# Keeping converted first-layer weight parts in DRAM and reading them back for the second token batch

## The chip, the cores and the metric

One core of a Trainium2 chip runs the kernel. The metric is device time in microseconds for one execution. Three runs of the kernel before took 870.82, 871.75 and 873.16 us; the median is 871.75 us.

## What is computed

Attention with a bucket mask (a key counts only where its six sign bits equal those of the query) over 2 batches, 8 heads, 768 positions of 64 numbers, and then two MLPs in a row on the 1536 x 512 result. Weights come as float64.

```python
q_bits = (np.einsum('bhsd,dk->bhsk', q, proj) > 0)      # k_bits alike; a bucket is its 6 bits
scores = np.where(q_bucket == k_bucket, scale * q @ k.T, -1e9)
attn = softmax(scores);  x = (attn @ v)                  # 1536 tokens x 512
h = x @ w_in;   x = (h * sigmoid(1.702 * h)) @ w_out     # first MLP,  512 -> 2048 -> 512
h = x @ w_in2;  out = (h * sigmoid(h)) @ w_out2          # second MLP, 512 -> 2048 -> 512
```

## The kernel before, in words

**Numbers.** TensorE works on float32r, so every operand is split into a high and a low part, and each product is three matmuls. The weights need more: they are float64, 8 bytes each, read as pairs of 32-bit words. For a block of 128 hidden units, `Weights.step` makes from the `raw` words a float32 tile `f` and then the parts `hi` and `lo`. That takes one ScalarE instruction (line 152), four VectorE instructions (lines 153, 154, 155, 157), a ScalarE copy that makes `hi` (line 159) and a GpSimd subtraction that makes `lo` (line 160). A block has kind "i" (128 columns of `w_in`) or "o" (128 rows of `w_out`); the two kinds of one block of hidden units form a place in the stream. A raw block is 512 KB, each of its two parts 256 KB.

**The stream of weights.** `order` lists 45 places: the 16 of the first MLP for the first token batch, then 13 of the same 16 again for the second batch (12 down to 0; the last three are still in SBUF), then the 16 of the second MLP. So 13 places, 26 blocks, are fetched and converted twice. Parts live in rings: `wpool` has room for 3 places, and once attention's memory is free, a pool `w2` for 6 more. A place's tiles can be written when the place that held them before has been used. `fetch` issues the transfer of a raw block on SP's queue (line 127), some blocks ahead; there are 2 raw tiles, 4 once attention is done.

**The stages.** Attention works through the heads in 96 steps, 48 for each batch. A step is the scores on TensorE, their minimum on VectorE (line 407), the exponential on ScalarE (412), a split into float16 parts (423 or 421, and 427 on GpSimd), and for every two steps one transposing DMA on SP (433, `pt<-hl`) whose result TensorE multiplies by v (445 to 447). Beside the second batch's attention the first MLP runs on the first batch's tokens (token blocks 0 and 1 of 384): `gemm1` is line 593, the gate (lines 598 to 604) is made on ScalarE, VectorE and GpSimd, `gemm2` is line 627, and its results are added up in `part` (634, 636). When attention is over, the first MLP runs on blocks 2 and 3 in units of places: the three that are still there, then 4, 4, 4 and 1. Then the second MLP takes all four blocks through units of four places.

**What sets the order.** The program calls its tasks in one order, each with a head start in instructions (`SOONER`), and a scheduler then writes each engine's instruction list. Every engine, and SP's queue too, takes its list strictly in order. DMA completions go round eight semaphores, and a new DMA waits until the eighth before it has landed.

Of the kernel before, what the change touches and what calls it, by code (L numbers as in the profile page):

```python
# [9 lines left out]
F32 = mybir.dt.float32  # L10
# [11 lines left out]
def tile_lsh_attention_two_mlps(  # L22
# [19 lines left out]
    P = 128  # L42
# [15 lines left out]
    # a float64's upper word, read as a float32: bounds for what float32 can hold  # L58
# [17 lines left out]
    # which steps' high parts VectorE makes, by batch  # L76
    HIGHV = ((5, (2, 4)), (3, (2,)))
    # how much sooner than in order the scheduler takes a task, in instructions:
    # first batch, second batch, rest
# [14 lines left out]
    # x, float32 = high + low, one tile for each block of tokens  # L94
# [3 lines left out]
    # ---------------------------------------------------------------- weights  # L98
    # A stream of float64 blocks, for 128 of the hidden units each: w_in's columns
    # ("i") and w_out's rows ("o"). A block becomes high + low parts that float32r  # L100
    # holds exactly; a place in the stream is one such pair of blocks.
# [3 lines left out]
    class Weights:  # L105
        def __init__(self, order, pool_of):
            self.order = order
            self.pool_of = pool_of
            self.chunks = [(i, kind) for i in range(len(order)) for kind in "io"]
            self.raw = {}  # L110
            self.t = {}
            self.issued = 0
            self.done = 0
            self.used = set()

        def fetch(self):
            i, kind = self.chunks[self.issued]
# [10 lines left out]
            self.raw[self.issued] = raw  # L128
            self.issued += 1
# [8 lines left out]
        def step(self):  # L138
# [7 lines left out]
            lo = pool.tile([P, NDC, P], F32R, tag=f"w{kind}l", name=f"w{kind}l")  # L146
            raw = self.raw.pop(n)
# [13 lines left out]
            self.t[i, kind] = hi, lo  # L161
            self.done += 1
# [7 lines left out]
    # -------------------------------------------------------------- attention  # L170
    def attention_setup(sp, s1, more, ps_m):
# [9 lines left out]
        # projection, split and laid out for the row blocks of a pair:  # L181
        # k of both heads, then q of both heads
# [3 lines left out]
        # (for each bit a row that is set and one that is clear, and a constant row)  # L186
        # high parts in columns from 0 on, low parts in columns from LOWC on
# [12 lines left out]
        # thresholds and weights of those rows  # L200
# [19 lines left out]
        # v of a pair; a column of ones beside the high part gives the row sums  # L220
# [5 lines left out]
    def attention(sp, s1, ps_m, ps_v, ahead_of, setup):  # L226
        nat, st = {}, {}
        # steps (head, queries), in groups; the last pair of a batch goes by halves
        # of the queries, so that the first half is ready sooner
# [30 lines left out]
        # Scores come negated, from -q / sqrt(D).  # L260
        # q as [low; high], k as [high; low]: their product is the two cross
        # terms; the product of the high parts comes with the bucket rows.
# [35 lines left out]
        # place of a head in BQ and BK: there is one more for the first batch  # L298
# [3 lines left out]
        # heads of a pair, by their places in BQ and BK  # L302
# [27 lines left out]
        # rows of the very first head, written in place  # L330
# [10 lines left out]
        # v, scaled by a power of two into float16's range, as high + low  # L341
# [53 lines left out]
        # tiles of a step; the first batch has room for more of them  # L395
# [7 lines left out]
        # negated scores, LOW where the buckets differ, and their minimum  # L403
# [10 lines left out]
        # high and low parts of two steps, turned by one DMA  # L414
# [34 lines left out]
        # x of the steps of a group, which are one head's  # L449
# [32 lines left out]
        # work on the next pair, by the step of the present one: (first, between, last)  # L482
# [23 lines left out]
        # the first pair, one head after the other  # L506
# [246 lines left out]
```

## Time and profile before

| what | value |
|---|---|
| runs | 870.82, 871.75, 873.16 us, median 871.75 |
| profiled execution | span 869.9 us from the first to the last instruction; its own time outside the span is not recorded apart, the three runs lie 0.9 to 3.3 us above it |
| TensorE matmul busy | 755.5 us, 87% of the span |
| VectorE busy | 650.6 us, 75% |
| GpSimd / ScalarE busy | 480.3 / 445.9 us |
| DMA | 102.78 MB, SP's queue 49.0% of 16 engines' span |

The shares of busy time are averages over stages with different limits, so the table says little alone. Attention with both batches reaches to about 425 us; the first MLP's second pass from there to about 605 us; the second MLP from there to the end.

### The profile page before, as it was taken

How to read it: one execution, taken by the hardware profiler on the slowest of the kernel's cores; microseconds unless marked ns; L12 is line 12 of the kernel's file. 1: busy time of each engine (PE TensorE's matmuls, PEld its weight loads, DVE VectorE, ACT ScalarE, POOL GpSimd, SP SyncE). 2: the span in 40 equal slices, each digit the busy share in tenths (PEclk: the TensorE clock that was granted, in tenths of full speed). 3: DMA queues.
4: the chain of work that ended last, by engine and by line, in shares of the span. 5: the costliest groups of instructions: out<-in, count | busy, mean ns of one | idle time of the engine just before them, and what ended most of it. 6: DMA issues, size and time to landing. Idle time of an engine off the chain costs nothing.

```text
span 869.9 us, 14004 instructions
## 1 busy us (share of the span) xinstructions
PE 755.5 (87%) x5332; PEld 691.0 (79%) x5332; DVE 650.6 (75%) x1091; ACT 445.9 (51%) x767; POOL 480.3 (55%) x360
## 2 busy tenths in 40 slices
PE   6666876679888988889998998867999999999998
PEld 4555765478888877789888898856998998998996
DVE  8796877999999999887689999898942753522222
ACT  6576876576666666565455444445543532322120
POOL 5466666777665865866655555557752633422121
PEclk9698989879998999999998999986999999999999
DMA  3789999997577566665533433243211310000011
GB/s 109 158 163 189 192 183 224 195 230 194 136 158 178 133 154 154 146 142 113 133 122 100 141 124 121 97 136 107 96 49 49 98 49 1 1 1 0 25 49 73
DMA packets 190031, 102.78 MB, mean 118 GB/s; under 512 B 152070, under 2 KB 181254, under 8 KB 189964
## 3 DMA queue, kind: packets, MB, share of 16 engines
q1 hardware_dynamic: 189804, 101.88, 49.0%
q8 instruction: 42, 0.69, 0.3%
q14 instruction: 25, 0.20, 0.1%
q10 hardware_dynamic: 160, 0.00, 0.0%
HBM read 56.63 MB, written 3.15 MB: 69 GB/s over the span
## 4 chain that ended last, share of the span: by engine, by line
PE 38%; DVE 36%; DMA 10%; issue 8%; ACT 3%; POOL 3%; SPq 2%; DVEq 0%; ACTq 0%; POOLq 0%
PE psh L593 18%; PE pso L627 17%; DVE f L155 7%; DVE f L157 5%; DMA pt<-hl 5%; DVE f L153 5%; DVE f L154 5%; DVE p L407 3%; DMA nk<-in_k_dram 3%; DVE part L636 2%; POOL hl L427 1%; DVE g L602 1%; DVE VS L377 1%; DMA raw<-in_moe_w_out_dram 1%; SPq L433 1%
## 5 line engine op out<-in xcount | busy, mean ns | idle before, releaser
L604 POOL TENSOR_TENSOR gl<-g,gh 128x384 fp32r<-128x384 f32 x128 | 145.0, 1134 | 160.2 <-ACT gh L603 135.5
L427 POOL TENSOR_TENSOR hl<-p,hl 128x768 f16<-128x768 f32 x96 | 170.7, 1786 | 100.3 <-ACT hl L423 47.2
L593 PE MATMUL psh<-XH,wih 128*128 128x384 f32 x512 | 176.3, 344 | 15.0 <-ACT wih L159 7.3
L593 PE MATMUL psh<-XH,wil 128*128 128x384 f32 x512 | 173.7, 339 | 1.5 <-POOL wil L160 1.5
L593 PE MATMUL psh<-XL,wih 128*128 128x384 f32 x512 | 173.5, 339 | 0.0
L636 DVE SCALAR_TENSOR_TENSOR part<-pso,part 128x384 f32<-128x384 f32 (+1 forms) x124 | 72.2, 589 | 62.5 <-PE pso L627 62.5
L627 PE MATMUL pso<-gh,woh 128*128 128x384 f32 x256 | 92.8, 369 | 25.3 <-DVE g L599 10.1
L593 PEld LDWEIGHTS psh<-XH,wih 128*128 128x128 f32 x512 | 98.0, 191 | 20.2 <-ACT wih L159 8.2
L412 ACT ACTIVATE p<-p,lo 128x768 f32<-128x768 f32 x96 | 89.6, 937 | 41.7 <-DVE p L407 41.1
L602 DVE TENSOR_TENSOR g<-g,psh 128x384 f32<-128x384 f32 x96 | 52.6, 549 | 74.8 <-ACT g L601 74.8
L603 ACT CAST gh<-g 128x384 fp32r<-128x384 f32 x128 | 65.5, 513 | 76.5 <-DVE g L602 67.9
L593 PEld LDWEIGHTS psh<-XH,wil 128*128 128x128 f32 x512 | 97.6, 191 | 2.4 <-POOL wil L160 2.2
L593 PEld LDWEIGHTS psh<-XL,wih 128*128 128x128 f32 x512 | 97.8, 191 | 0.6
L407 DVE TENSOR_SCALAR_CACHE_REDUCE p<-pss 128x768 f32<-128x768 f32 x96 | 90.6, 946 | 9.8 <-PE pss L390 7.7
L389 PE MATMUL pss<-ak,aq 128*128 128x384 f32 x192 | 76.4, 399 | 24.0 <-DVE p L407 23.8
L157 DVE SCALAR_TENSOR_TENSOR f<-raw,f 128x512 int32<-128x512 int32 x90 | 93.1, 1034 | 0.8
L160 POOL TENSOR_TENSOR wil<-f,wih 128x512 fp32r<-128x512 f32 x45 | 65.9, 1465 | 50.0 <-ACT wih L159 48.6
L627 PE MATMUL pso<-gl,woh 128*128 128x384 f32 x256 | 89.6, 350 | 3.8 <-POOL gl L604 3.8
L155 DVE SCALAR_TENSOR_TENSOR f<-raw,f 128x512 int32<-128x512 int32 x90 | 90.8, 1010 | 1.5
L627 PE MATMUL pso<-gh,wol 128*128 128x384 f32 x256 | 88.7, 347 | 0.0
L152 ACT ACTIVATE f<-raw 128x512 f32<-128x512 f32 x90 | 60.5, 673 | 49.5 <-POOL wil L160 18.2
L445 PE MATMUL pav<-VS,pt 128*128 128x65 f16 x576 | 64.9, 200 | 23.0 <-DMA pt<-hl 20.6
(112 smaller groups left out, 1712.3 us busy)
## 6 DMA issues: line engine op xcount, KB each, us to landing
raw<-in_moe_w_in_dram SPq DMA_DIRECT2D x45, 512.0 KB
raw<-in_moe_w_out_dram SPq DMA_DIRECT2D x45, 512.0 KB
nk<-in_k_dram SPq DMA_DIRECT2D x16, 192.0 KB
nq<-in_q_dram SPq DMA_DIRECT2D x16, 192.0 KB
nv<-in_v_dram SPq DMA_DIRECT2D x8, 384.0 KB
out_dram<-part SPq DMA_DIRECT2D x12, 256.0 KB
BQ<-aq SPq DMA_DIRECT2D x10, 192.0 KB
BK<-ak SPq DMA_DIRECT2D x6, 192.0 KB
```

The costliest lines, as they stand in the source:

```text
L155: V.scalar_tensor_tensor(out=fi, in0=top, scalar=-0x40000000, in1=fi, op0=ALU.bitwise_and, op1=ALU.bitwise_or)
L157: V.scalar_tensor_tensor(out=fi, in0=bot, scalar=29, in1=fi, op0=ALU.logical_shift_right, op1=ALU.bitwise_or)
L160: G.tensor_tensor(out=lo, in0=f, in1=hi.bitcast(F32), op=ALU.subtract)
L389: T.matmul(o, lhsT=lq, rhs=ak[:, half, :], start=True, stop=False)
L407: V.tensor_scalar(p, st.pop(("S", j)), LOW, None, op0=ALU.min, op1=ALU.min, accum_out=lo)
L412: A.activation(p, p, AF.Exp, bias=lo, scale=-1.0)
L427: G.tensor_tensor(out=hl[:, 1], in0=st.pop(("p", j))[0], in1=hl[:, 0], op=ALU.subtract)
L593: T.matmul(h, lhsT=a[:, c], rhs=x[t][:, c], start=(n == 0), stop=(n == 3 * NDC - 1))
L603: A.copy(gh[:, f], g)
L604: G.tensor_tensor(out=gl[:, f], in0=g, in1=gh[:, f].bitcast(F32), op=ALU.subtract)
L627: T.matmul(y, lhsT=a, rhs=x, start=(n == 0), stop=(n == 3 * nf - 1))
L636: V.scalar_tensor_tensor(out=acc, in0=y, scalar=scale, in1=acc, op0=ALU.mult, op1=ALU.add)
```

## The change

`Weights` learns which blocks come a second time (`last`, `again`). When such a block has been converted for the first time, both parts are copied from SBUF to two DRAM tiles (`spill`), 52 stores of 256 KB on SP's queue. When the block comes again, nothing is fetched and nothing converted: `fetch` skips it, and `step` issues two reads of 256 KB from the DRAM tiles straight into `hi` and `lo`. The rest of the program is called in the same order. (The diff also empties comment lines, which are left out here.)

```diff
     wpool = ctx.enter_context(tc.tile_pool(name="w", bufs=RING))
+    spill = ctx.enter_context(tc.tile_pool(name="spill", bufs=1, space=bass.MemoryType.DRAM))
...
+            self.last = {b: i for i, b in enumerate(order)}
+            self.kept = {}
+
+        def again(self, n):
+            i = self.chunks[n][0]
+            return self.order.index(self.order[i]) < i
 
         def fetch(self):
-            i, kind = self.chunks[self.issued]
+            n = self.issued
+            self.issued += 1
+            if self.again(n):
+                return
+            i, kind = self.chunks[n]
...
-            self.raw[self.issued] = raw
-            self.issued += 1
+            self.raw[n] = raw
...
+            block = self.order[i]
+            self.t[i, kind] = hi, lo
+            self.done += 1
+            if self.again(n):
+                for t, d in zip((hi, lo), self.kept.pop((block, kind))):
+                    SP.dma_start(out=t.bitcast(F32), in_=d)
+                return
             raw = self.raw.pop(n)
...
             G.tensor_tensor(out=lo, in0=f, in1=hi.bitcast(F32), op=ALU.subtract)
-            self.t[i, kind] = hi, lo
-            self.done += 1
+            if self.last[block] > i:
+                self.kept[block, kind] = []
+                for t, part in ((hi, "h"), (lo, "l")):
+                    d = spill.tile([P, NDC, P], F32, name=f"sp{kind}{part}{block[1]}")
+                    SP.dma_start(out=d, in_=t.bitcast(F32))
+                    self.kept[block, kind].append(d)
```

The scheduler writes new lists. Three places matter.

SP's queue while the second batch's attention begins, before. `raw` are weight blocks, `pt<-hl` the transposing DMAs of attention:

```order
L127 DMA raw_2072<-in_moe_w_in_dram 128x4x128
L433 DMA_TRANSPOSE pt_2251<-hl_2164 128x24x128
L127 DMA raw_2205<-in_moe_w_out_dram 128x512
L433 DMA_TRANSPOSE pt_2306<-hl_2248 128x24x128
L127 DMA raw_2308<-in_moe_w_in_dram 128x4x128
L433 DMA_TRANSPOSE pt_2636<-hl_2484 128x24x128
L127 DMA raw_2397<-in_moe_w_out_dram 128x512
```

The same place now; `spih`, `spil`, `spoh`, `spol` are the DRAM tiles of the high and low parts of kinds "i" and "o":

```order
L139 DMA raw_2078<-in_moe_w_in_dram 128x4x128
L455 DMA_TRANSPOSE pt_2177<-hl_2073 128x24x128
L183 DMA spil0_1950<-wil_1939 128x512
L183 DMA spoh0_2090<-woh_2080 128x512
L455 DMA_TRANSPOSE pt_2265<-hl_2174 128x24x128
L183 DMA spol0_2092<-wol_2081 128x512
L139 DMA raw_2215<-in_moe_w_out_dram 128x512
L183 DMA spih1_2227<-wih_2217 128x512
L455 DMA_TRANSPOSE pt_2320<-hl_2262 128x24x128
L183 DMA spil1_2229<-wil_2218 128x512
L139 DMA raw_2322<-in_moe_w_in_dram 128x4x128
L455 DMA_TRANSPOSE pt_2666<-hl_2510 128x24x128
```

Between two transposing DMAs there are now one fetch and about two stores, where there was one fetch. A store of a low part waits for GpSimd, as the transposing DMA behind it does.

VectorE where the second pass of the first MLP begins, before. `f` are the conversions, `g` the gate, `part` the sums:

```order
L154 TENSOR_SCALAR f_5794<-f_5794 128x512
L155 SCALAR_TENSOR_TENSOR f_5794<-raw_5756,f_5794 128x512
L602 TENSOR_TENSOR g_5751<-g_5751,psh_5738 128x384
L157 SCALAR_TENSOR_TENSOR f_5794<-raw_5756,f_5794 128x512
L153 TENSOR_SCALAR f_5824<-f_5824 128x512
L602 TENSOR_TENSOR g_5785<-g_5785,psh_5772 128x384
L154 TENSOR_SCALAR f_5824<-f_5824 128x512
L155 SCALAR_TENSOR_TENSOR f_5824<-raw_5758,f_5824 128x512
L602 TENSOR_TENSOR g_5815<-g_5815,psh_5802 128x384
L157 SCALAR_TENSOR_TENSOR f_5824<-raw_5758,f_5824 128x512
```

The same place now:

```order
L502 TENSOR_TENSOR XL_70<-psx,XH_66 128x384
L624 TENSOR_TENSOR g<-g,psh 128x384 x6
L171 TENSOR_SCALAR f<-f 128x512
L172 TENSOR_SCALAR f<-f 128x512
L624 TENSOR_TENSOR g<-g,psh 128x384
L173 SCALAR_TENSOR_TENSOR f<-raw,f 128x512
L171 TENSOR_SCALAR f<-f 128x512
L175 SCALAR_TENSOR_TENSOR f<-raw,f 128x512
```

Six gates stand together where conversions stood between them. The conversions that are left here are those of the second MLP's first blocks.

SP's queue behind the last transposing DMAs, before:

```order
L433 DMA_TRANSPOSE pt_5618<-hl_5553 128x24x128
L433 DMA_TRANSPOSE pt_5672<-hl_5615 128x24x128
L127 DMA raw_5756<-in_moe_w_out_dram 128x512
L127 DMA raw_5758<-in_moe_w_in_dram 128x4x128
L127 DMA raw_5760<-in_moe_w_out_dram 128x512
```

And now:

```order
L455 DMA_TRANSPOSE pt_5722<-hl_5657 128x24x128
L455 DMA_TRANSPOSE pt_5776<-hl_5719 128x24x128
L163 DMA wih_5860<-spih12_4122 128x512
L163 DMA wil_5861<-spil12_4124 128x512
L163 DMA woh_5882<-spoh12_4156 128x512
L163 DMA wol_5883<-spol12_4158 128x512
L163 DMA wih_5904<-spih11_3835 128x512
```

The reads of the second pass stand directly behind attention's last transposing DMAs, six places of four reads in a row.

## Rows read from the trace of the kernel before

**Rows 1.** Busy time of each engine by stretch: start and end us, length, then us busy (and instructions) of TensorE matmul, TensorE weight load, VectorE, ScalarE, GpSimd, and the granted TensorE clock, the DMA share, GB/s.

```profile
core 0: us, PE busy (x) PEld busy (x) DVE busy (x) ACT busy (x) POOL busy (x), PEclk, DMA share, GB/s
160.00:200.00 40.00, 30.41 (x296) 27.60 (x294) 38.98 (x64) 26.53 (x44) 29.15 (x19) 0.85 1.09 229
200.00:425.00 225.00, 200.38 (x1736) 186.43 (x1735) 202.97 (x350) 133.46 (x219) 153.36 (x104) 0.97 0.65 144
425.00:440.00 15.00, 13.89 (x80) 13.27 (x79) 13.30 (x19) 9.54 (x17) 9.81 (x8) 1.00 0.52 176
440.00:605.00 165.00, 139.83 (x731) 132.91 (x730) 152.49 (x209) 77.31 (x146) 92.87 (x72) 0.92 0.36 118
605.00:870.00 265.00, 261.16 (x1323) 237.64 (x1322) 114.62 (x176) 91.30 (x179) 98.68 (x87) 1.00 0.12 42
```

**Rows 2.** What TensorE's matmuls waited for from 440 to 605 us: us in total, times, longest us.

```profile
PE pso L627 <- ACT gh L603: 8.9, 4, 6.3
PE psh L593 <- ACT wih L159: 6.2, 2, 5.4
PE psh L593 <- DVE g L602: 4.8, 5, 1.9
PE pso L627 <- POOL gl L604: 3.8, 4, 1.6
PE psh L593 <- POOL wil L160: 1.0, 1, 1.0
```

**Rows 3.** VectorE's and two other engines' groups from 440 to 605 us: line, engine, operation, out<-in, shapes, count | us busy, mean ns | us idle before, and what ended it.

```profile
L155 DVE SCALAR_TENSOR_TENSOR f<-raw,f 128x512 int32<-128x512 int32 x38 | 41.0, 1079 | 0.9
L157 DVE SCALAR_TENSOR_TENSOR f<-raw,f 128x512 int32<-128x512 int32 x38 | 35.5, 934 | 0.5
L154 DVE TENSOR_SCALAR f<-f 128x512 int32<-128x512 int32 x37 | 32.5, 879 | 0.9
L153 DVE TENSOR_SCALAR f<-f 128x512 f32<-128x512 f32 x37 | 23.3, 631 | 9.5 <-ACT f L152 9.5
L602 DVE TENSOR_TENSOR g<-g,psh 128x384 f32<-128x384 f32 x31 | 16.9, 544 | 0.7 <-ACT g L601 0.7
L636 DVE SCALAR_TENSOR_TENSOR part<-pso,part 128x384 f32<-128x384 f32 x28 | 15.1, 548 | 0.0
L604 POOL TENSOR_TENSOR gl<-g,gh 128x384 fp32r<-128x384 f32 x31 | 36.9, 1193 | 28.0 <-ACT gh L603 16.3 <-issue 11.7
L603 ACT CAST gh<-g 128x384 fp32r<-128x384 f32 x31 | 15.9, 513 | 23.8 <-DVE g L602 23.7
L601 ACT ACTIVATE g<-psh 128x384 f32<-128x384 f32 x30 | 14.6, 485 | 1.6 <-PE psh L593 1.6
```

**Rows 4.** The chain of work that ended last, in order of time: start us, length us, what. The first row is a transfer at the end of attention, the last two are from the second MLP.

```profile
426.02 3.84 DMA raw<-in_moe_w_out_dram
...
642.89 8.34 PE psh L593 x48
651.24 8.20 PE pso L627 x36
```

**Rows 5.** TensorE's matmuls from 440 to 605 us by line (busy us, count), line 593 first and line 627 second.

```profile
440.00:605.00 165.00, 69.30 (x364) 65.23 (x364) 0.92 0.36 118
440.00:605.00 165.00, 73.55 (x367) 67.92 (x366) 0.92 0.36 118
```

**Rows 6.** DMA from 440 to 600 us, where weight blocks are nearly all that moves: SP's queue (packets, MB, share of 16 engines), and the issues.

```profile
q1 hardware_dynamic: 12096, 18.88, 36.1%
...
raw<-in_moe_w_in_dram SPq DMA_DIRECT2D x19, 512.0 KB
raw<-in_moe_w_out_dram SPq DMA_DIRECT2D x18, 512.0 KB
```

**Rows 7.** SP's queue in order of time: start us, us, line, kind, out<-in.

```profile
167.48 5.91 SPq L433 DMA_TRANSPOSE pt<-hl  x1
...
315.70 3.59 SPq L433 DMA_TRANSPOSE pt<-hl  x1
...
426.02 0.33 SPq L127 DMA_DIRECT2D raw<-in_moe_w_out_dram  x1
426.40 0.43 SPq L127 DMA_DIRECT2D raw<-in_moe_w_in_dram  x1
```

**Rows 8.** SP's issues of the two fetches and of the transposing DMA: count, ns min/median/max, first and last start us.

```profile
L127 SPq DMA_DIRECT2D raw<-in_moe_w_in_dram x45: 378/379/582, 147.2 to 696.7; - x45
L127 SPq DMA_DIRECT2D raw<-in_moe_w_out_dram x45: 327/328/526, 147.8 to 699.9; - x45
L433 SPq DMA_TRANSPOSE pt<-hl x48: 3578/4121/5912, 27.1 to 415.6; - x48
```

**Rows 9.** GpSimd's subtractions that make `lo`: count, ns min/median/max, first and last start us.

```profile
L160 POOL TENSOR_TENSOR wil<-f,wih x45: 1268/1466/2123, 160.8 to 746.6; 128x512 fp32r<-128x512 f32 x45
```

**Rows 10.** What TensorE's matmuls waited for from 200 to 430 us, attention's second batch: us in total, times, longest us.

```profile
PE pso L627 <- DVE g L599: 10.1, 8, 2.7
PE pso L627 <- DVE part L636: 4.3, 5, 1.4
PE pav L445 <- DMA pt<-hl: 3.8, 3, 1.4
```

## Prediction

> **What bounds the kernel now.** I read the busy time by stretch first [rows 1]. The reader is to see three regimes. From 200 to 425 us (second batch's attention beside the first MLP on the first batch) VectorE is busy 203.0 of 225 us and TensorE 200.4. From 440 to 605 us (first MLP on the second batch) VectorE is busy 152.5 of 165 us, TensorE 139.8 and its granted clock falls to 0.92. From 605 us on (second MLP) TensorE is busy until it stops, 261.2 us, at a clock of 1.00, while VectorE is below half.
>
> So only the middle stretch has room that this change can reach. The second view is what TensorE waited for there [rows 2]: 7.2 us for the parts of weights (6.2 + 1.0), 17.5 us for the gate (8.9 + 4.8 + 3.8). The gate waits are not a matter of the gate's own length. The third view, VectorE's groups in that stretch [rows 3], shows why: four conversion lines take 41.0 + 35.5 + 32.5 + 23.3 = 132.3 us, and the gate's own line 602 takes 16.9. VectorE takes its list in order, and a gate stands behind conversions in it. Both kinds of wait are VectorE's backlog.
>
> How long would TensorE need alone? All 731 matmuls of the stretch have 384 columns, 364 + 367 [rows 5]. In the second MLP, with TensorE never idle, 48 such matmuls take 8.34 us [rows 4], 0.17375 us each. 731 x 0.17375 = 127.0 us. The stretch took 165.0. **The gap is 38.0 us**: 25 us idle (165.0 - 139.8) and some 13 us in which matmuls ran at the lower of the two clock levels after such pauses.
>
> **The change part by part.**
>
> *Conversions removed.* 26 of the roughly 37 conversions of the stretch go. One costs VectorE 1.079 + 0.934 + 0.879 + 0.631 = 3.52 us [rows 3]. What is left for VectorE is about 12 conversions (the second MLP's first blocks, 42 us), the gate (16.9) and the sums (15.1): 74 us beside TensorE's 127.0. VectorE stops being the limit, and ScalarE (77.3 us) and GpSimd (92.9 us), which lose work as well, were below it already [rows 1]. TensorE is next. Credit: -38.0 us.
>
> *What stays of the gap.* Bounds: nothing, as from 605 us on, where conversions and gates also run and TensorE has no pause; and 17.5 us of gate waits plus their part of the lower clock, if they were inherent. I take +3 us, nearer to the first because the gate no longer stands behind conversions: one gate chain laid bare, at the short last unit of one place, is 0.485 + 0.544 + 0.513 + 1.193 = 2.7 us [rows 3].
>
> *Reads in place of fetches.* The bytes are the same: 512 KB of raw block become two parts of 256 KB. In the stretch 18.88 MB took 36.1% of all 16 DMA engines over 160 us [rows 6], that is 57.8 us of full DMA, 327 GB/s. A place (four reads, 1.05 MB) is then 3.2 us of DMA against 24 x 2 x 0.17375 = 8.3 us of TensorE for its two token blocks. The first reads are issued where the first raw fetch was, at 426.02 us, when attention's memory is free [rows 7]; that fetch landed after 3.84 us [rows 4]. TensorE at that time still has the three places that never left SBUF, 72 + 72 matmuls or 25 us. In the new list 24 reads for six places stand in a row, 19 us of DMA. Cost: 0, covered by these 25 us; without that cover, one landing, 3.84 us.
>
> *Conversions of the second MLP.* They come earlier but can't be written before a place's tiles are used up. After the gate inputs of the unit that frees the first four places, TensorE has 336 matmuls left in the first MLP, 58 us. Eight blocks at 3.52 us are 28 us of VectorE. Cost: 0.
>
> *Stores added.* 52 stores of 256 KB fall between about 160 and 425 us, on the queue that also issues attention's transposing DMAs, and this is the unknown. Three prices. Issue: a plain DMA holds SP 0.33 to 0.58 us [rows 8], so 52 take 17 to 30 us of SP. Order: in the new list seven transposing DMAs stand directly behind a store that waits for a `lo` which GpSimd makes just after the attention tile; at 1.47 us each [rows 9] that is 10 us of delay. Bandwidth: 13.6 MB at 327 GB/s are 42 us of full DMA over 265 us, 0.16 on top of a share of 0.65 [rows 1], so 0.81. On the path little of this counts so far: TensorE waited only 3.8 us for `pt` from 200 to 430 us [rows 10], since VectorE is the limit there and its list has conversions to do while others wait. Bounds: a small gain of 3 us, as the lists are written anew, though nothing is taken out of this stretch; and 40 us, issue and order all on the path. I take **+4 us**, close to the lower end: as much as is waited for `pt` now, once more.
>
> Here the Trainium skill speaks against the change. DMA: Bandwidth & Descriptors, in its rules for kernel authors, wants at least 1 MiB for each DMA, and puts a fixed cost of some 2.0 us on every one (Anatomy of one DMA), most of it the wait for the write's receipt, longest when the target is HBM, as it is for these stores. By its formula, as an estimate, a part of 256 KB takes 2.6 us, and four in a row 10.4 us for each place, more than TensorE's 8.3; 13 places would give back 27 us, for 868 us. The same page also says that fixed costs overlap when DMAs are issued early, and the list issues 24 at once; I therefore leave the sum at 0.
>
> **Sum.** 871.75 - 38.0 + 3 + 4 = 840.75, so **841 us**. The sum is made in the profiled execution, whose span is 869.9 us; the 1.85 us to the median of the runs is taken as unchanged.
>
> **The rivals.**
>
> *Stores slow attention, but mildly.* Transposing DMAs hold SP longer when DMA is crowded: 5.91 us where the share was 1.09, 3.59 us later [rows 1, 7]. If each of the 24 of the second batch lengthens by 0.8 us more on the path than I assume, the stage costs 20 us more: 861 us. For it: SP would be issuing for 24 x 4.1 + 52 x 0.4 = 119 of 225 us [rows 8]. Against: the share stays at 0.81.
>
> *The gate's waits are its own.* If the 17.5 us and their part of the lower clock (17.5 of 25, of 13 us, so 9) remain, 27 us come off the credit: 871.75 - 38 + 27 + 4 = 865 us. Against: 8.9 us of it are four waits, one of them 6.3 us long [rows 2], more than twice the chain of 2.7 us, and the stretch after 605 us has none.
>
> *Reads come one after another.* At best half of a raw block's 3.84 us for each, 7.7 us for a place, and TensorE would just be fed; at worst 3.84 each, 15.4 us, 13 x 7.1 = 92 us lost. Against: fetches were issued 0.4 us apart before one had landed [rows 7].
>
> *Slower: transposing DMAs end behind stores.* The place is SP's queue in the second batch's attention. If each of the 24 waits for one `lo` more (1.47 us) and for two stores' issue (2 x 0.43), and TensorE stands still for all of it, that is 2.3 x 24 = 56 us: 871.75 - 38 + 3 + 56 = 893 us. It decides from 35 / 24 = 1.5 us of added delay on the path for each transposing DMA. Against: the transposing DMA waits for GpSimd as well, in the same order but for those seven.
>
> *The change does nothing.* If TensorE's pauses had another cause than VectorE, the time stays at about 872 us. The idle column of VectorE [rows 3] speaks against it: under 1 us before three of its four conversion lines.
>
> **How the numbers follow.** My forecast with its bounds (831 to 850): 0.66. Mild slowing, around 861: 0.14. Gate waits remain, 865: 0.09. Serial reads: 0.03, half of it slower than before. Slower by the queue, 893: 0.05. Nothing: 0.03. The range runs from 871.75 - 38 - 3 = 831 to 862, with the first two cases and part of the third, about 0.82. A measurement of this kernel can tell about 0.3%, 2.6 us, from no change. Faster by more: 0.66 + 0.14 + 0.09 + 0.01 = 0.90; within it 0.04; slower 0.06.
>
> **What would show it.** Right: in the changed kernel's rows by stretch, the first MLP's second pass is as full of TensorE as the second MLP is, at a clock of 1.00, VectorE well below it; matmuls wait for neither `wih` nor `gh` for more than 3 us in all; attention ends between 422 and 430 us. Wrong in the third term: attention ends much later than 430 us, and `pav` waits for `pt` for far more than 3.8 us. Wrong in the second: waits for `gh` or `gl` remain. Wrong in the reads: matmuls wait for a DMA into `wih` or `woh`.

## The result and the profile after

| | before | after |
|---|---|---|
| median of 4 runs each, same chip | 871.51 us | 849.20 us (847.92 to 852.91) |
| ratio, 95% interval | | 0.9752 [0.9723, 0.9780] |
| span of the profiled execution | 869.9 us | 846.1 us (its time 847.92) |

Faster by 22.3 us; forecast were 841 (831 to 862), and 849.2 lies just inside the first case of the prediction (831 to 850). Lines of the new file lie 22 further down where matmuls and gates are (593 is 615, 602 is 624, 627 is 649), 18 in the conversions (157 is 175), 12 at the fetch (139). Reads are line 163, stores line 183.

Busy time by stretch, with the columns of [rows 1]; the last five rows are cut finer:

```profile
160.00:200.00 40.00, 32.62 (x332) 28.52 (x330) 36.27 (x63) 27.36 (x46) 26.99 (x18) 0.93 1.12 263
200.00:425.00 225.00, 195.92 (x1674) 181.42 (x1673) 202.13 (x345) 130.22 (x216) 145.34 (x101) 0.96 0.78 191
425.00:440.00 15.00, 11.37 (x87) 10.72 (x86) 4.40 (x10) 4.40 (x8) 7.60 (x8) 0.89 0.58 151
440.00:605.00 165.00, 160.70 (x899) 158.84 (x899) 95.99 (x143) 67.98 (x135) 74.47 (x64) 0.98 0.42 144
605.00:846.00 241.00, 237.26 (x1198) 215.28 (x1196) 93.76 (x150) 77.33 (x151) 81.03 (x73) 1.00 0.11 36
...
440.00:470.00 30.00, 30.00 (x175) 30.00 (x175) 11.84 (x18) 14.11 (x30) 10.32 (x10) 1.00 0.88 319
470.00:500.00 30.00, 30.00 (x175) 30.00 (x174) 7.75 (x14) 8.54 (x17) 8.06 (x8) 1.00 0.36 124
...
540.00:560.00 20.00, 20.00 (x117) 20.00 (x117) 18.96 (x28) 9.01 (x17) 11.86 (x9) 1.00 0.35 114
560.00:580.00 20.00, 15.70 (x75) 15.38 (x74) 17.99 (x28) 8.75 (x16) 11.62 (x11) 0.83 0.38 124
580.00:600.00 20.00, 20.00 (x105) 18.46 (x104) 18.36 (x24) 9.95 (x20) 15.90 (x13) 1.00 0.24 80
```

From 440 to 605 us VectorE fell from 152.5 us [rows 1] to 96.0, and TensorE rose from 731 matmuls to 899. It is full from 440 to 560 us and has one hole, in 560 to 580, where VectorE is busy 18.0 of 20 us. Two things are not as forecast: that hole, and the first row, where VectorE has 36.3 us in place of 39.0.

Matmuls' waits in the second pass (against [rows 2]: five kinds, 24.7 us) are down to one row:

```profile
PE pso L649 <- ACT gh L625: 4.3, 1, 4.3
```

VectorE's conversions in that stretch, with the columns of [rows 3], 18 where there were 38:

```profile
L175 DVE SCALAR_TENSOR_TENSOR f<-raw,f 128x512 int32<-128x512 int32 x18 | 19.1, 1062 | 0.1
L173 DVE SCALAR_TENSOR_TENSOR f<-raw,f 128x512 int32<-128x512 int32 x18 | 17.5, 973 | 0.4
L171 DVE TENSOR_SCALAR f<-f 128x512 f32<-128x512 f32 x19 | 14.2, 748 | 7.1 <-ACT f L170 7.1
L172 DVE TENSOR_SCALAR f<-f 128x512 int32<-128x512 int32 x18 | 12.3, 684 | 0.4
```

The reads, in SP's queue, and what DMA moved from 440 to 600 us in 40 slices of 4 us:

```profile
434.26 0.33 SPq L163 DMA_DIRECT2D wih<-spih  x1
434.63 0.43 SPq L163 DMA_DIRECT2D wil<-spil  x1
...
444.62 0.32 SPq L163 DMA_DIRECT2D woh<-spoh  x1
445.31 0.32 SPq L163 DMA_DIRECT2D wol<-spol  x1
```

```profile
GB/s 389 390 387 369 388 251 219 136 321 346 118 6 0 0 0 74 311 143 131 83 48 0 4 0 0 105 157 2 214 89 184 146 26 131 131 89 46 120 63 82
```

Reads are issued 0.4 to 0.5 us apart and later 0.68 us, which for 256 KB is 385 GB/s, nearly what the first three slices show (387 to 390; from 452 us on raw blocks of the second MLP are among them). They follow one another at the highest rate of these slices, and no matmul waits for them.

**Two numbers for each run.** To compare kernels I cut each profile at the end of the last `pav`, attention's product with v; `pso` is the result of `gemm2`. Behind it every kernel has at least 1536 matmuls of 384 columns at 0.17375 us and 576 of 512 columns at 0.2278 (8.20 us for 36), both from [rows 4]: 398.1 us. Some have 6 to 30 matmuls of the first batch's MLP left as well; these count as work of the attention stage. So **A** is the end of the last `pav` plus 0.17375 us for each of those, and the **gap** is the time from there to the last `pso`, less 398.1. Before: A 423.45 + 24 x 0.17375 = 427.6, gap 40.5. After: A 432.65, gap 11.5. The change gained 28.9 us in the gap and gave back 5.0 in A; 23.9 together, and the spans differ by 23.8.

| run | stores | median us (ratio, interval) | A | gap | VectorE busy 160 to 240 us |
|---|---|---|---|---|---|
| before | none | 871.5 | 427.6 | 40.5 | 76.1 |
| b1_before_scores | none | 871.0 (0.9997 [0.9979, 1.0016]) | 429.2 | 38.2 | 75.0 |
| e1_no_stores | 4 | 845.8 (0.9709 [0.9677, 0.9742]) | 432.7 | 9.6 | 73.5 |
| e12_late_stores | 36, late | 849.2 (0.9755 [0.9733, 0.9776]) | 430.5 | 15.0 | 76.5 |
| e9_half | 26 | 851.3 (0.9759 [0.9731, 0.9786]) | 433.1 | 15.0 | 72.0 |
| after | 52 | 849.2 (0.9752 [0.9723, 0.9780]) | 432.7 | 11.5 | 70.7 |
| e7_cut | 52 | 852.3 (0.9778 [0.9756, 0.9801]) | 437.9 | 12.3 | 72.1 |
| e6_scores_sooner | 52 | 845.4 (0.9707 [0.9679, 0.9736]) | 433.0 | 7.9 | 68.3 |
| e2_stores_alone | 52 | 882.2 (1.0114 [1.0073, 1.0156]) | 434.1 | 38.8 | 72.5 |
| e3_thin_stores | 52, 32 KB | 855.4 (0.9824 [0.9796, 0.9852]) | 440.5 | 11.0 | 71.8 |
| e4_stores_act | 52, ScalarE | 851.3 (0.9771 [0.9744, 0.9799]) | 439.2 | 8.4 | 69.0 |
| e11_one_dma | 26, 512 KB | 854.5 (0.9803 [0.9773, 0.9833]) | 439.0 | 12.7 | 72.3 |
| e10_double | 104 | 869.2 (0.9968 [0.9945, 0.9991]) | 454.4 | 11.7 | 61.6 |
| e5_stores_pool | 52, GpSimd | 880.3 (1.0097 [1.0062, 1.0131]) | 466.9 | 11.5 | 63.1 |

A, gap and the last column come from one profiled execution each; that of e2 took 876.5 us, 5.7 less than e2's median. The kernel after and e7 have the same lists up to the second pass and differ by 5.2 us in A, so a difference of a few us in A between two rows proves nothing; groups of rows do.

### The profile page after: what moved, and what is told of

It reads as the page before. It is cut to its first block, busy times and chain, and to the rows that moved or that the text cites. A ratio compares the mean times of both kernels' runs of the same rounds, so it can differ in the third digit from the quotient of the medians.

```text
span 846.1 us, 13926 instructions
## 1 busy us (share of the span) xinstructions
PE 751.1 (89%) x5332; PEld 691.8 (82%) x5332; DVE 561.4 (66%) x987; ACT 415.9 (49%) x715; POOL 434.2 (51%) x334
## 4 chain that ended last, share of the span: by engine, by line
PE 57%; DVE 21%; DMA 9%; issue 6%; ACT 4%; POOL 2%; SPq 1%; DVEq 0%; POOLq 0%
PE pso L649 27%; PE psh L615 26%; DMA pt<-hl 5%; DVE p L429 3%; DMA nk<-in_k_dram 3%; DVE f L171 3%; DVE f L173 2%; DVE f L175 2%; DVE VS L399 1%; DVE hl L443 1%; POOL hl L449 1%; DVE f L172 1%; DVE part L658 1%; DVE g L621 1%; PE pss L411 1%
## 5 line engine op out<-in xcount | busy, mean ns | idle before, releaser
L626 POOL TENSOR_TENSOR gl<-g,gh 128x384 fp32r<-128x384 f32 x128 | 141.0, 1102 | 218.8 <-ACT gh L625 206.7
L449 POOL TENSOR_TENSOR hl<-p,hl 128x768 f16<-128x768 f32 x96 | 168.0, 1757 | 81.4 <-ACT hl L445 38.0
L649 PE MATMUL pso<-gh,woh 128*128 128x384 f32 x256 | 90.4, 359 | 22.4 <-DVE g L621 12.4
L623 ACT ACTIVATE g<-psh 128x384 f32<-128x384 f32 x96 | 46.8, 489 | 97.8 <-PE psh L615 96.8
L467 PEld LDWEIGHTS <-pt 128*128 128x128 f16 x576 | 55.2, 101 | 29.9 <-DMA pt<-hl 24.8
L649 PE MATMUL pso<-wol,gh 128*128 128x512 f32 x192 | 75.0, 391 | 0.0
L649 PE MATMUL pso<-woh,gh 128*128 128x512 f32 x192 | 74.7, 389 | 0.0
```

What stands on the lines that cost most here:

```text
L449: G.tensor_tensor(out=hl[:, 1], in0=st.pop(("p", j))[0], in1=hl[:, 0], op=ALU.subtract)
L467: T.matmul(o, lhsT=pt[:, i], rhs=hv, start=(i == 0), stop=False)
L623: A.activation(g, h, AF.Sigmoid, scale=beta)
L626: G.tensor_tensor(out=gl[:, f], in0=g, in1=gh[:, f].bitcast(F32), op=ALU.subtract)
L649: T.matmul(y, lhsT=a, rhs=x, start=(n == 0), stop=(n == 3 * nf - 1))
```

## Experiments

The question that the result leaves is where A's 5 us (8.2 us at the first read, 434.26 against 426.02) came from, and the gap's 11.5. Theories of the first: the redrawn instruction list (ORDER), the stores' place on SyncE (QUEUE), their bytes (BYTES).

**e1_no_stores**: four stores left; every read takes the parts of block 0.

```diff
-            if self.last[block] > i:
-                self.kept[block, kind] = []
+            if self.last[block] > i and block[1] == 0:
+                self.kept["one", kind] = []
...
-                for t, d in zip((hi, lo), self.kept.pop((block, kind))):
+                for t, d in zip((hi, lo), self.kept["one", kind]):
...
-                    self.kept[block, kind].append(d)
+                    self.kept["one", kind].append(d)
```

> Only the four parts of block 0 are stored (4 stores in place of 52); every read of the second token batch takes those four parts, so the other blocks' products are left out. Three theories of why the last step of attention comes 8.2 us later with the change (first read issued at 434.3 us, where the first fetch was issued at 426.0 before). ORDER: the scheduler wrote the list anew, and 13 attention steps are left on VectorE after the 28th conversion where there were 10 (7 against 4 after the 32nd), at some 2.7 us for each; in this kernel's list the counts are 10 and 4 again, so the first read is issued at 426 us and the time is 841 us. QUEUE: 48 stores fewer are issued on SyncE; first read at 426 to 427, 841 us. BYTES: 12.6 MB fewer; the same, 426 to 427, 841 us. If the delay has nothing to do with the stores or the list they cause, it stays at 434, 849 us. The second pass (last pav to the second MLP) should in each case keep the 11.5 us that it now takes above its matmuls' own time.

The first read came at 431.1 us, A is 432.7: neither 426 nor 434, and no theory had it. Nearly all stores are gone and A is that of the change, so A alone does not show that the 52 stores are what makes it later. The gap stayed, 9.6.

**e2_stores_alone**: stores, but no reads.

```diff
         def again(self, n):
-            i = self.chunks[n][0]
-            return self.order.index(self.order[i]) < i
+            return False
```

> All 52 stores are made, and the second token batch fetches and converts its blocks again as before the change: the cost of the stores alone. VectorE's list is that of the changed kernel for its first 490 rows, and 13 attention steps are left after the 28th conversion. ORDER, QUEUE and BYTES all expect attention to end some 8 us later than before (first fetch of the second pass at 432 to 435 us) and the gap of the second pass to be back at some 40 us: 871.5 + 8 = 879 us. If the changed kernel lost its 8 us to something the reads do, attention ends at 426 and the time is 871.5 us.

The first fetch came at 435.9 us, as all expected, and the gap is back at 38.8. Matmuls wait there again as in [rows 2]:

```profile
PE pso L648 <- ACT gh L624: 8.0, 2, 7.3
PE pso L648 <- POOL gl L625: 3.3, 4, 1.2
PE psh L614 <- DVE g L623: 3.2, 3, 2.2
PE psh L614 <- POOL wil L177: 2.2, 2, 1.3
PE psh L614 <- ACT wih L176: 2.2, 2, 1.9
```

So the stores, with the list that the scheduler writes for them, cost 1.1% here, and the gain is all in not converting again.

**e3_thin_stores**: an eighth of the bytes.

```diff
-                for t, d in zip((hi, lo), self.kept.pop((block, kind))):
+                for t, d in zip((hi, lo), self.kept[(0, 0), kind]):
...
-                    SP.dma_start(out=d, in_=t.bitcast(F32))
+                    p = P if block[1] == 0 else 16
+                    SP.dma_start(out=d[0:p], in_=t[0:p].bitcast(F32))
```

> All 52 stores are issued in the same places, but those of blocks 1 to 12 take 16 of 128 partitions, 32 KB in place of 256 KB; reads are whole and take block 0's parts, so the other blocks' products are left out. QUEUE: SyncE issues as many stores, so the first read stays at 434 us, time 849 us. BYTES: 11 MB fewer, first read at 427 us, time 842 us. ORDER: 12 steps are left after the 28th conversion and 6 after the 32nd, so 426.0 + 2 x 2.7 = 431.5 us, time 846 to 847 us.

First read at 442.1 us, later than with whole stores and than any theory had it, though DMA's share from 160 to 240 us fell from 1.03 to 0.89 (rows below). So the bytes alone do not make A late. This kernel's extra 7.8 us of A aren't VectorE standing idle either: from 100 us to the last step of attention it took 297.9 us for 512 instructions, where 515 took 290.4 with the change (columns as in [rows 1]; before, after, e3). Why they took longer stays open.

```profile
100.00:423.70 323.70, 273.55 (x2553) 251.21 (x2551) 289.29 (x510) 201.87 (x325) 221.21 (x146) 0.94 0.78 165
```

```profile
100.00:433.00 333.00, 279.04 (x2568) 254.49 (x2564) 290.35 (x515) 202.81 (x329) 220.78 (x150) 0.94 0.86 200
```

```profile
100.00:440.80 340.80, 280.64 (x2544) 252.35 (x2543) 297.91 (x512) 202.00 (x328) 216.79 (x149) 0.93 0.74 163
```

**e6_scores_sooner**: all stores, another list.

```diff
-    SOONER = (..., {'scores': 200, ...
+    SOONER = (..., {'scores': 300, ...
```

> The changed kernel with all its stores and reads; one number of the scheduler's priorities for the second batch, scores, is 300 in place of 200, which redraws the list: 8 attention steps are left on VectorE after the 28th conversion (13 in the changed kernel, 10 before) and none after the 32nd. ORDER: the tail is shorter by some 5 steps of 2.7 us, first read at 421 us, time 836 us. QUEUE and BYTES: the stores are the same, so 434 us and 849 us. If conversions now come too late for the first MLP instead, TensorE waits for wih or woh before 430 us and nothing is gained.

First read at 430.4 us, A 433.0: neither the 421 of ORDER's count of steps nor the 434 of QUEUE and BYTES. The 3.9 us that it gained on the kernel after lie in the gap (7.9): 30 matmuls of the first batch were left to fill the entry to the second pass. It has the best median of all runs, but its interval overlaps that of the change.

**b1_before_scores**: the same number changed in the kernel before (no stores).

```diff
-    SOONER = (..., {'scores': 200, ...
+    SOONER = (..., {'scores': 300, ...
```

> The kernel before the change, without any store, with the scheduler's priority of scores in the second batch at 300 in place of 200: nothing but the list is redrawn. ORDER: the list of the kernel before is a lucky draw; a redrawn one ends attention some 3 to 8 us later, first fetch of the second pass at 429 to 434 us, time 874 to 880 us. STORES: without stores attention ends at 426 to 427 us whatever the draw, time 871.5 us, within 2 us.

Ratio 0.9997, first fetch at 427.8 us, A 429.2. This redraw costs nothing that can be measured, so ORDER, as I had put it, falls too; that another redraw could cost something isn't excluded by one.

**e10_double**: every store twice.

```diff
                     SP.dma_start(out=d, in_=t.bitcast(F32))
+                    d2 = spill.tile([P, NDC, P], F32, name=f"sq{kind}{part}{block[1]}")
+                    SP.dma_start(out=d2, in_=t.bitcast(F32))
```

> Every store is made twice, to two places in DRAM: 104 stores and 27 MB more written than before the change, 52 stores and 13.6 MB more than with it. QUEUE: 52 more issues at 0.33 to 0.58 us hold SyncE for 17 to 30 us more; if the stores cost attention its 8 us, it ends some 8 us later still, first read at 442 us, 857 us. BYTES: the same, or more, as DMA's share of 200 to 425 us goes from 0.78 towards 0.93. ORDER: the list is redrawn, and its draw alone decides: anywhere from 426 to 442 us (where the runs with none, 4, 52 and 52 thin stores lay, in no order of their stores).

First read at 456.3 us, A 454.4, 22 us more: far outside the spread of the lists, and beyond the 442 us of QUEUE. Stores do have a price: for the second 52 it is four times the 5.0 us by which the change lies behind the kernel before.

**e4_stores_act** and **e5_stores_pool**: other queues.

```diff
-                    SP.dma_start(out=d, in_=t.bitcast(F32))
+                    A.dma_start(out=d, in_=t.bitcast(F32))     # e4; e5: G.dma_start
```

> The 52 stores are issued on ScalarE in place of SyncE; reads stay on SyncE. So far VectorE's idle time from 100 us to the last step of attention grows with the number of stores on SyncE, whatever their size: 33 and 35 us with none (two lists), 36 with 4, 40 to 43 with 26 or 52, 41 with 52 thin ones, 64 with 104. QUEUE: the stores hold the queue that attention's transposing and loading DMAs need; with SyncE free of them VectorE's idle time falls to 33 to 37 us and the first read comes at 428 to 431 us, time 844 to 846 us. BYTES: the same 13.6 MB are written, idle time 40 to 43 us, 433 to 438 us. A third way: ScalarE takes its list in order too, and a store of a low part waits there for GpSimd with exponentials and gate functions behind it; then waits for exponentials and g grow, 26 times about 1.5 us at most, and the time is 850 us or more.

> The 52 stores are issued on GpSimd, right behind its subtraction that makes the low part, so no store waits for another engine for long. QUEUE: VectorE idle 33 to 37 us up to the last step of attention, first read at 428 to 431 us, 844 to 846 us. BYTES: idle 40 to 43, 433 to 438 us, 849 to 854 us. ORDER: 14 attention steps are left after the 28th conversion (13 with the change, 10 before) and 9 after the 32nd: 437 us or later. If issuing a DMA costs GpSimd much, its own low parts come late, matmuls wait for wil, wol and gl, and the time is above 855 us.

With no store on SyncE, A is 439.2 (e4), no better than with them there, so QUEUE's gain isn't borne out. But more than SyncE's time is different in e4: its matmuls waited 11.7 us for `pt` from 200 to 430 us, where those of the change waited 0.9. Its time, 851.3 us, fits the third way, but that way's sign, longer waits for exponentials and `g`, did not show: from 160 to 425 us VectorE waited 3.2 us for `g` and 2.7 for exponentials, with the change 5.5 and 2.2. On GpSimd A is 466.9, 34 us later; first row e5, second the kernel after (ns min/median/max):

```profile
L183 POOL DMA_DIRECT2D spih<-wih x13: 557/557/688, 160.2 to 371.1; - x13
```

```profile
L183 SPq DMA_DIRECT2D spih<-wih x13: 320/437/535, 155.5 to 343.5; - x13
```

52 issues at 0.557 us are 29 us of GpSimd. The expectation had matmuls wait for `wil`, `wol` and `gl`; no such wait shows. They waited for `pt`, the transposed `hl` that GpSimd makes: 27.3 us from 160 to 468 us, against 3.1 with the change:

```profile
PE pav L467 <- DMA pt<-hl: 27.3, 11, 5.1
```

**e11_one_dma**: 26 stores and 26 reads of 512 KB.

```diff
-            hi = pool.tile([P, NDC, P], F32R, tag=f"w{kind}h", name=f"w{kind}h")
-            lo = pool.tile([P, NDC, P], F32R, tag=f"w{kind}l", name=f"w{kind}l")
+            both = pool.tile([P, 2, NDC, P], F32R, tag=f"w{kind}", name=f"w{kind}")
+            hi, lo = both[:, 0], both[:, 1]
...
-                for t, d in zip((hi, lo), self.kept.pop((block, kind))):
-                    SP.dma_start(out=t.bitcast(F32), in_=d)
+                SP.dma_start(out=both.bitcast(F32), in_=self.kept.pop((block, kind)))
...
-                self.kept[block, kind] = []
-                for t, part in ((hi, "h"), (lo, "l")):
-                    d = spill.tile([P, NDC, P], F32, name=f"sp{kind}{part}{block[1]}")
-                    SP.dma_start(out=d, in_=t.bitcast(F32))
-                    self.kept[block, kind].append(d)
+                d = spill.tile([P, 2, NDC, P], F32, name=f"sp{kind}{block[1]}")
+                SP.dma_start(out=d, in_=both.bitcast(F32))
+                self.kept[block, kind] = d
```

> High and low part of a block lie in one tile, which is stored by one DMA of 512 KB and read back by one: 26 stores and 26 reads in place of 52 and 52, the same bytes. By the rule that larger DMAs are better (DMA: Bandwidth & Descriptors, of the Trainium skill) it should gain wherever a fixed cost of each DMA is on the path. QUEUE: half the issues, so VectorE's idle time falls from 40 to some 37 us and the first read comes 3 to 4 us earlier, at 431 us, time 846 us. BYTES: no change there, 849 us. Second pass: reads are covered, so its gap stays at 8 to 12 us; if landings were on its path it would shrink, or grow where the first matmul must now wait for both parts (3 to 4 us at 435 us).

First read at 441.0 us, A 439.0, gap 12.7, 854.5 us: no gain from larger DMAs on either side. QUEUE had 431 us and 846, BYTES 849.

**e12_late_stores**: no stores before 215 us, while DMA is fullest.

```diff
-            return self.order.index(self.order[i]) < i
+            return self.order[i][1] >= 4 and self.order.index(self.order[i]) < i
...
-            if self.last[block] > i:
+            if self.last[block] > i and block[1] >= 4:
...
-    again = [NF - 1 - RING - i for i in range(NF - RING)]
+    again = [3, 2, 1, 0] + list(range(NF - RING - 1, 3, -1))
```

> Blocks 0 to 3, which are converted from 150 to 215 us while DMA is busiest, are not stored; they are fetched and converted again in the second pass, and come first there, where VectorE is busy only 12 of 30 us (440 to 470) and 8 of 30 (470 to 500). 36 stores and 36 reads are left of 52 and 52. EARLY: what the stores cost attention they cost where DMA is full, since in every run with 52 stores VectorE lost 1.5 to 6 us of busy time from 160 to 200 us against the kernel before, and the later ones are free: VectorE's idle time from 100 us to the last step of attention is back at 33 to 36 us (40 to 46 with 52 stores, 33 and 35 with none), attention ends 5 us earlier (first read or fetch of the second pass at 427 to 430 us), the 8 conversions (28 us of VectorE) are covered, and the time is 843 to 845 us. ANYWHERE: the later stores cost as much, idle 39 to 42 us, 848 to 851 us. If the first matmuls of the second pass wait for the fetched blocks in spite of the 25 us of matmuls ahead of them, the gap of the pass rises above 15 us and the time above 850 us.

Busy time from 160 to 240 us, columns as in [rows 1], each row a kernel of its own: before, after, e3, e4, e10, e12.

```profile
160.00:240.00 80.00, 65.93 (x606) 60.68 (x603) 76.11 (x120) 50.37 (x86) 58.50 (x38) 0.91 0.86 189
```

```profile
160.00:240.00 80.00, 66.91 (x643) 59.83 (x641) 70.65 (x119) 50.83 (x86) 54.71 (x37) 0.97 1.03 249
```

```profile
160.00:240.00 80.00, 67.16 (x632) 60.19 (x632) 71.77 (x118) 49.71 (x85) 54.33 (x37) 0.91 0.89 206
```

```profile
160.00:240.00 80.00, 63.16 (x578) 58.57 (x576) 68.98 (x113) 48.77 (x82) 51.43 (x36) 0.89 1.07 239
```

```profile
160.00:240.00 80.00, 60.08 (x524) 53.02 (x521) 61.64 (x105) 47.44 (x80) 45.26 (x32) 0.94 1.07 267
```

```profile
160.00:240.00 80.00, 64.59 (x603) 57.75 (x601) 76.53 (x121) 50.02 (x86) 57.70 (x38) 0.94 0.88 203
```

The third number is VectorE's, the limit of that stretch. Without stores before 215 us it is 75.0 to 76.5 us (before, b1, and e12, which has 6 stores in this stretch where the change has 19); with any before that, even the four of e1, 61.6 to 73.5. Of A, e12 got back 2.2 us of the change's 5.0 (430.5), less than half of what EARLY expected and less than two executions of one list can differ by, and its first fetch came at 432.4 where EARLY had 427 to 430; its idle measure, VectorE's pauses of over 0.15 us summed from 100 us to the last `ri` (the scale of attention's result, in its last step), is 38.5, between EARLY's 36 and ANYWHERE's 39. The first matmuls of the pass waited 1.1 us for a converted block, and the gap is 15.0. What A gained the gap lost: 849.2 us.

**What is settled of A, and what is open.** With the change the attention stage is 5.0 us longer. That its 52 stores are what makes it so is not shown by A: e1 with four stores has the same A, and the two executions of one list, the kernel after and e7, differ by 5.2. Three things speak for the stores. Twice as many cost 22 us more (e10). VectorE's idle measure rises with them: 33.1 and 34.8 us with none, 36.4 with four, 38.5 with the 36 late ones, 42.5 and 42.8 with 26, 40.5 to 48.1 with 52 on SyncE or ScalarE (41.0 with the thin ones), 64.3 with 104. (The expectation of e4 gives 40 to 43 with 26 or 52; it leaves out e6, which has 48.1.) And from 160 to 240 us VectorE is less busy in every kernel that stores before 215 us (rows above). Fewer bytes (e3) and a SyncE free of stores (e4) did not bring A back, nor did one redraw of the list without stores cost anything (b1). What it is of a store stays open.

One candidate would fit e3 and e4: every DMA, on SyncE and on ScalarE, takes the next of the eight completion semaphores and waits until the eighth before it has landed, so a store of any size on either queue stands ahead of loads and transposes. The traces speak against it. Of SyncE's waits from 160 to 425 us none ended with a DMA's landing in the change, nor in e3 and e10; in e4 two did, 1.4 us in all:

```profile
SPq L455 <- DMA spol<-wol: 0.9, 1, 0.9
SPq L267 <- DMA pt<-hl: 0.5, 1, 0.5
```

**e7_cut** and **e9_half** ask what is left of the gap.

```diff
-    cut = [list(range(i, min(i + 4, len(order) - NF))) for i in range(NF, NF + len(again), 4)]
+    cut = [list(range(NF + i, NF + j)) for i, j in ((0, 4), (4, 7), (7, 10), (10, 13))]
```

> The changed kernel with the last 13 places of the second pass cut into units of 4, 3, 3, 3 in place of 4, 4, 4, 1. Every list is that of the changed kernel up to the second pass, so attention should end where it did (first read at 434.3 us). UNIT: the 4.3 us wait for gh at 572 us, which every run with the reads shows, comes from the unit of one place: between its last psh and its first pso of the second block TensorE has only 12 matmuls, 2.1 us, while sigmoid, product and copy stand between conversions of the second MLP on ScalarE and VectorE. With three places it has 36, 6.3 us; the wait and the slow matmuls behind it go, the gap of the second pass (time from the last pav to the end less its matmuls' own time) falls from 11.5 to some 5.5 us, time 843 us. BACKLOG: the conversions of the second MLP are bunched there whatever the units are, so a wait of about 4 us stays, perhaps in another unit: 849 us.

The gap is 12.3 us: BACKLOG. Without the short unit the wait was split over others, and the matmuls' waits from 440 to 605 us still sum as much:

```profile
PE pso L649 <- ACT gh L625: 4.3, 2, 3.2
PE pso L649 <- POOL gl L626: 1.2, 2, 0.8
```

```diff
-            i = self.chunks[n][0]
-            return self.order.index(self.order[i]) < i
+            i, kind = self.chunks[n]
+            return kind == "o" and self.order.index(self.order[i]) < i
...
-            if self.last[block] > i:
+            if kind == "o" and self.last[block] > i:
```

> Only the parts of w_out are kept and read; those of w_in are fetched and converted again in the second pass, so 13 conversions of the 26 come back (46 us of VectorE) and 26 stores go. ROOM: VectorE would be busy some 96 + 46 = 142 of the 165 us from 440 on, at most as much as TensorE, so most of the gain stays: gap 12 to 18 us, against 11.5 with all parts kept and 40.6 with none. SHARE: each conversion taken away gives the same, so the gap is half way, 26 us. Time, if attention ends as with the change: 849 to 855 us by ROOM, 864 us by SHARE.

The gap is 15.0 us: ROOM. With 13 conversions back VectorE is busy 133.4 us, and TensorE hardly notices:

```profile
440.00:605.00 165.00, 159.13 (x884) 156.81 (x883) 133.38 (x188) 77.33 (x151) 93.24 (x75) 0.97 0.41 137
```

Half the conversions taken away gave 25.5 of the 28.9 us of the gap. The gain came from getting VectorE below TensorE, not from each conversion. Nor did it come from ScalarE and GpSimd, which lose work with each conversion as well: here they are busy 77.3 and 93.2 us, as before the change (77.3 and 92.9 [rows 1]), and the gap went all the same.

## Why the prediction was right, and where its sizes were off

The forecast missed the median by 8.2 us: 6.1 in the gap, 1.0 in the stores, 1.3 because the profiled execution after was the fastest of its four, less 0.2 that the sum was rounded up.

**The credit of the gap** was right. It rested on VectorE's backlog in [rows 2, 3]; without the second conversion it went (after), with it it came back though all stores were made (e2). As forecast, all of the middle stretch's matmuls then ran at 0.174 us but for two places.

**What stays of the gap: +3, measured 11.5.** 3.9 us lie at the entry (last `pav` to 440 us) and 7.3 us between 560 and 580; elsewhere the gap is within 0.3 us of zero. The prediction's sign for this term, less than 3 us of waits for `wih` and `gh`, was missed by these 4.3. The step that failed is the one that costed the second MLP's conversions at 0, as 28 us of VectorE beside 58 us of TensorE. On average that is room, though less than forecast: 18 conversions fell into the stretch where about 12 were expected, and VectorE was busy 96.0 us where 74 were. But they are bunched where places come free, VectorE is busy 18 to 19 of every 20 us from 540 to 600, and the gate of the last unit stands in two lists behind them. ScalarE, VectorE and TensorE in the kernel after, start and length:

```profile
567.36 0.67 ACT L170 ACTIVATE f<-raw 128x512 f32<-128x512 f32 x1 [0.88 <-POOL wil L178]
568.59 0.67 ACT L170 ACTIVATE f<-raw 128x512 f32<-128x512 f32 x1 [0.56 <-POOL wol L178]
569.16 0.48 ACT L623 ACTIVATE g<-psh 128x384 f32<-128x384 f32 x1
571.29 0.62 ACT L177 CAST woh<-f 128x512 fp32r<-128x512 f32 x1 [1.65 <-DVE f L175]
571.82 0.51 ACT L625 CAST gh<-g 128x384 fp32r<-128x384 f32 x1
```

```profile
569.64 0.68 DVE L173 SCALAR_TENSOR_TENSOR f<-raw,f 128x512 int32<-128x512 int32 x1
570.24 0.42 DVE L172 TENSOR_SCALAR f<-f 128x512 int32<-128x512 int32 x1
570.58 0.68 DVE L175 SCALAR_TENSOR_TENSOR f<-raw,f 128x512 int32<-128x512 int32 x1
571.18 0.55 DVE L624 TENSOR_TENSOR g<-g,psh 128x384 f32<-128x384 f32 x1
```

```profile
567.74 0.34 PE L649 MATMUL pso<-gh,wol 128*128 128x384 f32 x1
572.38 1.65 PE L649 MATMUL pso<-gh,woh 128*128 128x384 f32 x4 [4.30 <-ACT gh L625]
573.82 0.53 PE L615 MATMUL psh<-XH,wih 128*128 128x384 f32 x1
```

The sigmoid (623) stands behind two conversions' first steps that wait for GpSimd, the product (624) behind three conversion steps, the copy (625) behind another copy: from sigmoid to `pso` 3.2 us, on top of a late start. TensorE stands for 4.3 us, and 3.0 more go in matmuls at the lower level behind it, which start 0.32 us apart in place of 0.174; the granted clock is 0.83 from 560 to 580 us. The place was forecast (the short last unit), as a chain of 2.7 us laid bare. But it isn't the shortness (e7). The rows above put it down to the conversions and to GpSimd, for which ScalarE waits; no run moved them, so this is argued and not shown.

**Reads at 0** was right, for all 52. A place's four reads took 4 x 0.68 = 2.7 us against TensorE's 8.3, close to the 3.2 worked out from [rows 6], and no matmul waited. The estimate by the Trainium skill's formula for one DMA (DMA: Bandwidth & Descriptors, Anatomy of one DMA, where it is fitted on DMAs that GpSimd issues; these are SyncE's) was 2.6 us for each and 868 us if they add up. Here they overlapped, and one DMA of 512 KB for two did not help (e11). The same page's rules for kernel authors say that the fixed setup cost of a DMA overlaps when it is issued early and waited for late, and the trace agrees: reads 0.68 us apart, no matmul waiting.

**Stores at +4**: the stage was 5.0 us longer, inside the bounds, but that is near the forecast by luck, since the way that was priced isn't the way it went, and with four stores the stage was as long (e1). Matmuls waited for `pt` less, not more: 0.9 us where [rows 10] has 3.8, from 200 to 430 us (2.4 up to 440 us, as attention ends later here):

```profile
PE pso L649 <- DVE g L621: 12.4, 11, 4.1
PE pso L649 <- DVE part L658: 5.6, 3, 2.7
...
PE pav L467 <- DMA pt<-hl: 0.9, 3, 0.4
```

VectorE lost the time, 76.1 to 70.7 us from 160 to 240 us, before most of the stores were made. My sign for this term, attention's end at 422 to 430 us, came out wrong: 434.3. Of those 8.2 us, 4.2 are 24 matmuls that were done earlier than before.

**The rivals.** Mild slowing (+20 on the stage) and transposes behind stores (893) did not happen with 52 stores on SyncE. The first came near in size with 104 (A 454.4, 22 us beyond the change), but not by its way alone: matmuls waited 7.8 us for `pt` there from 200 us to the end of attention. Gate waits inherent: no, 4.3 us of 17.5 remain. Serial reads: no. That the change does nothing: no.

## What to carry to other kernels

When work is taken off the limiting engine, the gain ends when the next engine is full: half of this change gave nearly nine tenths of it. The work that remains should be costed where it is bunched and by what stands behind it in each in-order list, not by its average over the stretch. Stores that nobody waits for aren't free: 104 of them cost 22 us more than 52, though what 52 cost is no larger than the spread of one list. Keeping them out of the fullest stretch brought VectorE's busy time back there but not the total (e12), and on GpSimd, whose results attention waits for, they cost more than the whole change gains (e5).

## What the runs showed of the hardware that was not expected

A DMA issued on GpSimd held it 0.54 to 0.73 us, and 52 of them made the kernel 31 us slower than the same ones on SyncE (880.3 against 849.2), while on ScalarE they made it 2.1 us slower (851.3), which is within the spread. Reads of 256 KB, queued 0.68 us apart, ran at 387 to 390 GB/s from 440 to 452 us, above the 327 GB/s worked out from the fetches of [rows 6]. A pause of TensorE of 4.3 us cost 7.3 us in all. Two executions of the same instruction lists had VectorE busy 290.4 and 294.3 us in the attention stage from 100 us on (the kernel after, to 433.0 us, and e7, to 438.1).
